# Reordering the edges of an attention stage: two weight loads earlier, the third output's rounding inside the second projection, the first output's columns inside the third

## The chip, the cores and the metric

The kernel runs on one NeuronCore of one Trainium2 chip. The metric is the time of one execution on the device in microseconds (us), as the median of three runs; lower is better. The core's engines work in parallel, each through its own queue in order: TensorE (PE) multiplies matrices and transposes, VectorE (DVE) and GpSimd (POOL) do elementwise arithmetic, ScalarE (ACT) does exponentials and copies and issues some DMAs, and SyncE (SP) issues most DMAs.

## The reference

One transformer block on x (2048 x 512, float32), modulated by a vector c. `A` is an attention with a memory: 32 heads of 16, in 4 segments of 512 rows, causal within a segment, and mixed by `g` with what a linear memory M, z of the earlier segments gives. `B` is a bilinear unit of inner width 1376.

```python
mod = (_silu(c) @ w_mod).reshape(1, 6, 1, -1)
sa, ca, ga, sb, cb, gb = (mod[:, i] for i in range(6))
h = _layernorm(x) * (1 + ca) + sa
x = x + ga * A(h, wq, wk, wv, wo, beta)
h = _layernorm(x) * (1 + cb) + sb
x = x + gb * ((h @ w_gate) * (h @ w_up)) @ w_down
# A, for each segment s with queries qs, keys ks, values vs of each head:
p = _softmax(qs @ ks.T * scale + causal_mask)
o = g * (phi(qs) @ M) / (phi(qs) @ z + 1e-6) + (1 - g) * (p @ vs)
M, z = M + phi(ks).T @ vs, z + phi(ks).sum()
# the segments' o, joined, @ wo
```

## The kernel before

**Precision.** A float32 operand of a projection is split into a rounded high part and the low part that is left (names in H and L: `wkH`, `wkL`, `ahH`, `ahL`, `oH`, `oL`), and three matmuls (high x high, low x high, high x low) make one product. Rounding is a copy on ScalarE, the low part a subtraction on VectorE or GpSimd. Queries and keys are split into three bfloat16 pieces, written to DRAM (`qd`, `kd`) and loaded again in another layout (`qst`, `kst`).

**The attention loop.** The 32 heads are 4 groups of 8, each group two units of 4 heads, so the 4 segments make 32 units u. A turn v of the loop has five slots. In each slot stand a q step of a later unit (scores q on PE, row maxima nm on VectorE), a filling, and a k step of unit v (transposed scores k on PE, exponential pt on ScalarE, and the causal mask on pt as affine selects on GpSimd); in one slot, av_step multiplies the previous unit's pt by v (`tb`), copied out as `tsb` and written to `td`. Later turns load the rows (`orow`) and denominators (`rd`, then `rb`), multiply, add the memory's part `memb` from the second segment on (`o_step`) and write `od`. The maxima nm go through the split nh and the transpose ntp to nt, which a DMA on ScalarE's queue adds to qst before the unit's k steps.

**The filling.** `fill` spends a credit per slot on two generators: `fill_a` (layer norms, weights, projections of queries, keys and values, the memory, the first output projection) and `fill_b` (output projections of segments 1 to 3, the second layer norm's columns, and the first gate and up weights). `weave(a, b, at)` runs a and puts steps of b behind the steps of a that `at` counts. A step that yields a number costs that much credit, and False ends the slot's filling. The instructions' order on PE is written out by hand in this way; most others are pinned behind the PE instruction issued last, and all engines keep the compiled order.

**What the change touches.** `load_g` loads the group g columns of wq or wk (`wrq`, `wrk`) into a staging buffer whose tag `stage` names, and on its second step rounds them. `a_kq` multiplies them with a segment's normalised columns (`kps`, `qps`). `wo_load` loads a segment's od into `orl`; `wo_op` rounds it to `oH` and subtracts to the low part `oL`, in orl's own place; `wo_mm` projects (`wops`), adds x (`xr`) and writes `x1d`. `lnC` loads x1d rows as `x1`, finds mean and factor (`cmv`, `cy`, refined in four small steps on GpSimd), normalises x1 in place and transposes it by columns (`ctp`), which ScalarE copies as `chf`; for the first segment they are split at once (`chH`, `chL`). `prep` loads gate and up weights (`w`) and forms their sums and parts (`AH`, `AL`). The last group of the last segment takes another way, by transposes `tr` of tsb, without DRAM. The first, second and third outputs are the attention outputs of segments 0, 1 and 2 (orl0, orl1, orl2 as loaded), and their rows on the way through projection and second norm. After the loop come the products of the bilinear unit (`g`) and the down projection (`acc`).

## Time and profile before

| | |
|---|---|
| median of 3 runs | 868.59 us (866.88 to 870.31) |
| profiled execution | 865.84 us, of it the span 864.0 us |
| PE busy | 827.9 us, 96% of the span |
| VectorE, ScalarE, GpSimd busy | 652.1, 473.7 and 422.7 us |
| mean granted clock of PE | 0.995 |
| first attention turn to last | about 39 to 505 us |
| products of the bilinear unit, down projection | about 515 us to the end |

The profile is of one execution, on the hardware; times in it are from the start of the span. The page gives busy shares and the chain of work that ended last, followed back from the last instruction. Rows in order of time show the start, the duration, the instruction with what it writes and reads (buffer numbers left out), and in square brackets how long the engine had stood idle and what ended that. PE is full in most stretches, so what counts is where it stands, and what it stands for.

### The profile page before, as it was taken

The numbers are of one execution on the slowest core, as the hardware profiler recorded it, in microseconds if no ns is written. First come the engines' busy times: TensorE is split into PE (matmuls) and PEld (weight loads), VectorE is DVE, ScalarE is ACT, GpSimd is POOL, SyncE is SP. The second block draws the span as 40 slices with busy tenths as digits, with TensorE's granted clock in tenths as the row PEclk, the third lists the DMA queues.
The fourth block names the chain that finished last, engine by engine and source line by source line (L and its number), as shares of the span: only waits on it lengthen the run. The fifth ranks groups of instructions, "written<-read, shape, count | busy, mean of one in ns | idle before, by whom it ended". The sixth has DMA issues, their size and how long they took to land.

```text
span 864.0 us, 14347 instructions
## 1 busy us (share of the span) xinstructions
PE 827.9 (96%) x4823; PEld 580.5 (67%) x4824; DVE 652.1 (75%) x1730; ACT 473.7 (55%) x740; POOL 422.7 (49%) x562
## 2 busy tenths in 40 slices
PE   8979999999999999989997999999999999999998
PEld 5746566556665566555654567888778888887886
DVE  8688678988779777789898878888785667667532
ACT  3747867698668875577545663333364333323321
POOL 4535744577346753586314806998101855550000
PEclk9999999999999999999999999999999999999999
DMA  7773748477566655967894453563315241122032
GB/s 244 233 199 123 229 154 229 151 251 245 159 200 207 214 187 167 271 221 215 253 280 158 148 171 114 168 182 117 107 31 168 74 123 49 50 56 95 0 119 98
DMA packets 111355, 139.45 MB, mean 161 GB/s; under 512 B 18800, under 2 KB 70000, under 8 KB 111280
## 3 DMA queue, kind: packets, MB, share of 16 engines
q1 hardware_dynamic: 106016, 130.91, 49.4%
q10 hardware_dynamic: 5264, 7.62, 2.4%
q8 instruction: 38, 0.62, 0.3%
q14 instruction: 37, 0.30, 0.1%
HBM read 87.48 MB, written 50.76 MB: 160 GB/s over the span
## 4 chain that ended last, share of the span: by engine, by line
PE 70%; DMA 8%; DVE 8%; ACT 6%; POOL 5%; issue 3%; SPq 1%; ACTq 0%; POOLq 0%; DVEq 0%
PE g L90 24%; PE acc L90 14%; PE tb L90 6%; PE k L90 5%; PE q L90 5%; PE vps L90 4%; DVE q L40 3%; PE wops L90 3%; PE kps L90 3%; PE qps L90 3%; ACT pt L338 2%; DMA qd<-q 1%; DMA orl<-od 1%; DMA qst<-nt 1%; DMA memb<-memd 1%
## 5 line engine op out<-in xcount | busy, mean ns | idle before, releaser
L40 DVE CUSTOM_DVE_ANT_0 q<-q,cmask 128x384 f32<-128x384 f32 (+3 forms) x512 | 246.7, 508 | 56.2 <-PE q L90 46.1
L338 ACT ACTIVATE pt<-k 128x1024 f32<-128x1024 f32 x160 | 163.9, 1025 | 66.7 <-PE k L90 54.7
L341 POOL TENSOR_SCALAR_AFFINE_SELECT pt<-pt 128x256 f32<-128x256 f32 (+1 forms) x224 | 106.3, 488 | 143.5 <-ACT pt L338 138.9
L90 PE MATMUL q<-kst,qst 96*128 96x384 bf16 (+3 forms) x512 | 101.3, 300 | 8.4 <-DVE nm L40 7.4
L90 PE MATMUL k<-qst,kst 98*128 98x384 bf16 (+3 forms) x512 | 97.5, 302 | 7.8 <-ACT pt L338 7.3
L457 POOL TENSOR_TENSOR w<-w 128x256 f32<-128x256 f32 (+1 forms) x84 | 72.5, 875 | 65.9 <-DVE t L1228 37.9
L452 POOL TENSOR_TENSOR AL<-w,AH 128x512 fp32r<-128x512 f32 (+1 forms) x42 | 58.8, 1403 | 46.4 <-ACT AH L448 46.4
L90 PE MATMUL tb<-pt,v 128*32 128x512 f32 (+3 forms) x1024 | 75.7, 436 | 0.6 <-POOL pt L341 0.6
L90 PEld LDWEIGHTS <-kst 98*128 98x128 bf16 x512 | 38.2, 99 | 53.1 <-issue 46.0
L40 DVE DVE_READ_ACCUMULATOR2_ANT nm<- 128x1 f32 x512 | 72.1, 141 | 0.0
L448 ACT ACTIVATE AH<-w 128x512 fp32r<-128x512 f32 (+3 forms) x88 | 47.3, 565 | 43.3 <-POOL w L457 30.1
L90 PEld LDWEIGHTS <-qst 96*128 96x128 bf16 x512 | 43.4, 98 | 36.4 <-issue 11.6
L1485 DVE TENSOR_TENSOR mL<-mid,mH 128x512 fp32r<-128x512 f32 (+1 forms) x44 | 32.3, 738 | 41.5 <-ACT mH L1484 41.5
L90 PE MATMUL acc<-DH,mL 128*128 128x512 f32 x144 | 56.6, 393 | 0.9 <-DVE mL L1485 0.9
L90 PE MATMUL acc<-DH,mH 128*128 128x512 f32 x144 | 57.1, 397 | 0.0
L90 PE MATMUL acc<-DL,mH 128*128 128x512 f32 x144 | 56.5, 393 | 0.0
L1484 ACT ACTIVATE mH<-mid 128x512 fp32r<-128x512 f32 (+1 forms) x44 | 27.1, 627 | 51.7 <-PE acc L90 50.5
L90 PEld LDWEIGHTS tb<-pt,v 128*32 128x32 f32 x1024 | 28.6, 109 | 39.3 <-issue 34.5
L1277 ACT ACTIVATE p<-g 128x512 f32<-128x512 f32 (+1 forms) x22 | 13.1, 597 | 74.3 <-PE g L90 74.3
L452 DVE TENSOR_TENSOR AL<-w,AH 128x512 fp32r<-128x512 f32 (+3 forms) x44 | 32.6, 743 | 14.0 <-ACT AH L448 13.9
L367 ACT ACTIVATE tsb<-tb 128x512 f32<-128x512 f32 x32 | 19.1, 596 | 31.8 <-PE tb L90 31.7
L90 PE MATMUL g<-chH,AH 128*128 128x512 f32 (+1 forms) x88 | 34.8, 395 | 0.7 <-ACT p L1277 0.7
(286 smaller groups left out, 2054.6 us busy)
## 6 DMA issues: line engine op xcount, KB each, us to landing
kst<-kd SPq DMA_DIRECT2D x32, 384.0 KB
qst<-qd SPq DMA_DIRECT2D x32, 384.0 KB
td<-tsb ACTq DMA_DIRECT2D x28, 256.0 KB
wm<-in_w_mod_dram SPq DMA_DIRECT2D x24, 256.0 KB
kd<-k SPq DMA_DIRECT2D x16, 384.0 KB
qd<-q SPq DMA_DIRECT2D x16, 384.0 KB
w<-in_w_gate_dram SPq DMA_DIRECT2D x20, 256.0 KB
w<-in_w_up_dram SPq DMA_DIRECT2D x40, 128.0 KB
```

Source lines behind the costliest of these rows:

```text
L40: i = getattr(self.eng, name)(*a, **k)
L90: return pe(nc.tensor.matmul(*a, **k))
L338: lpt[0] = act.activation(pt, kp, AF.Exp, scale=0.25)
L341: sels[u, i] = nc.gpsimd.affine_select(w, w, pattern=[[0, w.shape[1]], [1, P]], compare_op=ALU.is_ge, fill=0.0, base=0, channel_multiplier=-1)
L367: act.activation(tsbs[u], tbs.pop(u), AF.Copy)
L448: i = act.activation(hi[sl], w[sl], AF.Copy)
L452: i = eng.tensor_sub(lo[sl], w[sl], hi[sl].bitcast(F32))
L457: i = ce.tensor_tensor(w[:, o, :, 0:n], w[:, x, :, 0:n], w[:, y, :, 0:n], op=op)
L1277: lcp[0] = act.activation(r["p1"], ps, AF.Copy)
L1484: pin(act.activation(mH[0:n], md[0:n], AF.Copy))
L1485: vec.tensor_sub(mL[0:n], md[0:n], mH[0:n].bitcast(F32))
```

## The change

Four things are changed. The loads of group 3's key and query weights are issued right behind those of group 1, before the attention loop, instead of inside it; the order of staging tags follows, so each weight keeps its buffer's tag. The first key projection of segments 1 to 3 takes all three products of columns 0 to 2 ahead of those of column 3, where it took all low columns last. The segment 3 sum of orow and memb is made by VectorE instead of GpSimd (groups 0 and 1; the two last groups had it there). And `fill_b` is woven anew: the third output's load, rounding and low parts move into the second projection, the low parts from VectorE to GpSimd, and the first output's columns move into the third projection, with the third and fourth columns of each no longer ending a slot.

```diff
--- before.py
+++ after.py
@@ -235,8 +235,6 @@
             if kept_h is not None:
                 kept_h.append(h)
             yield 0.45
-            if pfx == "c" and d % 2 == 1:
-                yield False
         return hH, hL
 
     def run(gen):
@@ -424,7 +422,7 @@
         if i == 0:
             pin(vec.tensor_mul(o, o, rds.pop(ug)))
             if s > 0:
-                nc.gpsimd.tensor_add(o, o, mems.pop(ug))
+                (vec if s == NSEG - 1 else nc.gpsimd).tensor_add(o, o, mems.pop(ug))
             return
         pin(nc.sync.dma_start(od[s][g], o))
         if g == NG - 1:
@@ -486,7 +484,7 @@
         prev = ()
 
         def sub(oL, a, oH):
-            pin(vec.tensor_sub(oL, a, oH.bitcast(F32)))
+            pin((nc.gpsimd if s == 2 else vec).tensor_sub(oL, a, oH.bitcast(F32)))
 
         def half(nm):
             if s % 2 == 0 or g == NG - 1:
@@ -697,7 +695,7 @@
                 i += 1
 
     wH, wL = {}, {}
-    stage = [("ph", 3), ("ph", 3), ("ph", 3), ("mem", 2), ("pkr", 1), ("f", 2)] + [("x", 4)] * 4 + [("mem", 2)] * 2
+    stage = [("ph", 3), ("ph", 3), ("ph", 3), ("mem", 2), ("pkr", 1), ("f", 2)] + [("x", 4)] * 2 + [("mem", 2)] * 2 + [("x", 4)] * 2
     nst = [0]
 
     def staged(nm):
@@ -775,7 +773,7 @@
             ps = bank(f"{nm}ps{s}_{g}")
             terms = [(k, a, b) for k in range(KT) for a, b in ((wH, hH), (wL, hH), (wH, hL))]
             if s > 0 and g == 0 and nm == "k":
-                terms.sort(key=lambda t: t[2] is hL)
+                terms.sort(key=lambda t: (t[0] == KT - 1, t[2] is hL))
             for n, (k, a, b) in enumerate(terms):
                 MM(ps, a[nm, g][:, k, :], b[k], start=n == 0, stop=n == 11)
                 if n in (2, 5, 8):
@@ -1000,10 +998,7 @@
                 ws = []
                 if s == 0 and g == 2:
                     xts[1] = xload(1)
-                if s == 0 and g < 3:
-                    ws = [load_g(nm, w, g + 1) for nm, w in (("k", wk_), ("q", wq))]
-                for w in ws:
-                    next(w)
+                    ws = w3
                 K, Q = a_kq(s, g, "k"), a_kq(s, g, "q")
                 if s == 0 and g == 2:
                     lns = a_ln(1)
@@ -1051,19 +1046,36 @@
         pr = prep(0, "0_0", bc, 1, pb, 1)
         op = wo_op(1, pb, o1, us[1])
         yield from weave(rest, op, (4, 5, 6, 7))
-        B["o0"] = True
-        lg = lnC(0, pb, bc, pb, "x1", 4)
+        lg, o2 = lnC(0, pb, bc, pb, "x1", 4), third(pb)
         rest = weave(wo_mm(1, us[1], xr_load(1, pb, (0,)), pb=pb), chain(op, islice(lg, 10)),
-                     (0, 1, 4, 5, 6, 7, 8, 11, 12, 13, 14))
-        yield from weave(rest, islice(pr, 1), (10,))
+                     (0, 1, 4, 5, 6, 7, 7, 10, 11, 12, 13))
+        rest = weave(rest, chain(o0_free(), islice(pr, 1)), (6, 14))
+        yield from weave(rest, o2, (11, 12, 13, 14, 15))
         while "o2" not in B:
             yield None
-        yield from weave(kept_as("nxt", lg), wo_op(2, pb, B["o2"], us[2]), (0, 1, 2, 3, 3))
+        yield from o2
         B["orl_free"] = True
-        lg = lnC(1, pb, bc, pb, "x1", 4)
-        rest = weave(wo_mm(2, us[2], xr_load(2, pb, (0,)), pb=pb), lg, (0, 3, 4, 5, 6, 7, 10, 11, 12, 13))
-        yield from weave(rest, pr, (1, 8, 9, 14))
-        B["hf"] = yield from lg
+        lh = weaved(kept_as("nxt", lg), pb, bc)
+        rest = weave(wo_mm(2, us[2], xr_load(2, pb, (0,)), pb=pb), lh, (0, 1, 2, 3, 3, 4, 7, 8, 9, 9, 10, 13, 14, 14, 15))
+        yield from weave(rest, pr, (10, 12, 18, 20))
+        B["hf"] = yield from lh
+
+    def weaved(lg, pb, bc):
+
+        yield from lg
+        yield 0.0
+        return (yield from lnC(1, pb, bc, pb, "x1", 4))
+
+    def third(pb):
+
+        while "o2" not in B:
+            yield 0.0
+        yield from wo_op(2, pb, B["o2"], us[2])
+
+    def o0_free():
+
+        B["o0"] = True
+        yield 0.0
 
     def kept_as(nm, g):
         B[nm] = yield from g
@@ -1117,8 +1129,8 @@
         pass
     next(lw[2])
     next(lw[2])
-    w1 = [load_g(nm, w, 1) for nm, w in (("k", wk_), ("q", wq))]
-    for w in w1:
+    w1, w3 = ([load_g(nm, w, g) for nm, w in (("k", wk_), ("q", wq))] for g in (1, 3))
+    for w in w1 + w3:
         next(w)
     run(kq0[1])
     run(kq0[0])
```

SP's queue ahead of the first loads of keys, where wrk and wrq are the weights by group, kd and qd the pieces in DRAM and kst the loaded keys. Before:

```order
L717 DMA wrk1_491<-in_wk_dram 128x4x128
L717 DMA wrq1_495<-in_wq_dram 128x4x128
L805 DMA kd0_0_107<-k3_0_0_478 128x512
L805 DMA kd0_0_107<-k3_0_0_478 128x2x512
L805 DMA kd0_0_107<-k3_0_0_478 128x3x512
L808 DMA qd0_0_91<-q3_0_0_514 128x3x512
L717 DMA wrk2_562<-in_wk_dram 128x4x128
L274 DMA kst0_224<-kd0_0_107 96x2048
L717 DMA wrq2_566<-in_wq_dram 128x4x128
```

Now:

```order
L715 DMA wrk1_491<-in_wk_dram 128x4x128
L715 DMA wrq1_495<-in_wq_dram 128x4x128
L715 DMA wrk3_499<-in_wk_dram 128x4x128
L715 DMA wrq3_503<-in_wq_dram 128x4x128
L803 DMA kd0_0_107<-k3_0_0_478 128x512
L803 DMA kd0_0_107<-k3_0_0_478 128x2x512
L803 DMA kd0_0_107<-k3_0_0_478 128x3x512
L806 DMA qd0_0_91<-q3_0_0_522 128x3x512
L715 DMA wrk2_570<-in_wk_dram 128x4x128
L715 DMA wrq2_574<-in_wq_dram 128x4x128
L272 DMA kst0_224<-kd0_0_107 96x2048
```

Group 3's loads (wrk3, wrq3) stand ahead of all pieces of group 0, and the first kst load stands behind both loads of group 2. Two dozen rows further on, wrk3 and wrq3 are gone from between the loads of qst2 and kst3.

ScalarE's queue around the k steps of units 28 and 29, where orl2 is the third output as loaded and oH2 its rounding, csd0 and cy0 the factor of the first output's rows and chf0 and ctp0 its columns. Before:

```order
L338 ACTIVATE pt28_3_6029<-k28_3_6024 128x1024
L181 ACTIVATE csd0_6010<-cmv0_5898,epst_74 128x4
L183 ACTIVATE cy0_6012<-csd0_6010 128x4
L338 ACTIVATE pt28_4_6056<-k28_4_6051 128x1024
L338 ACTIVATE pt29_0_6083<-k29_0_6080 128x1024
L367 ACTIVATE tsb28_6113<-tb28_6096 128x512
L338 ACTIVATE pt29_1_6120<-k29_1_6117 128x1024
L338 ACTIVATE pt29_2_6143<-k29_2_6138 128x1024
L318 DMA qst2_230<-nt30_6149 2x16x128
L506 ACTIVATE oH2_0_6180<-orl2_0_5848 128x512
L209 ACTIVATE chf0_0_6169<-ctp0_0_6170,modc_83 128x512
L506 ACTIVATE oH2_1_6220<-orl2_1_5850 128x512
```

Now:

```order
L336 ACTIVATE pt28_3_6029<-k28_3_6024 128x1024
L504 ACTIVATE oH2_0_6044<-orl2_0_5993 128x512
L181 ACTIVATE csd0_6004<-cmv0_5890,epst_74 128x4
L183 ACTIVATE cy0_6006<-csd0_6004 128x4
L336 ACTIVATE pt28_4_6055<-k28_4_6050 128x1024
L504 ACTIVATE oH2_1_6068<-orl2_1_5995 128x512
L504 ACTIVATE oH2_2_6078<-orl2_2_5997 128x512
L336 ACTIVATE pt29_0_6088<-k29_0_6085 128x1024
L365 ACTIVATE tsb28_6118<-tb28_6101 128x512
L336 ACTIVATE pt29_1_6125<-k29_1_6122 128x1024
L336 ACTIVATE pt29_2_6155<-k29_2_6150 128x1024
L316 DMA qst2_230<-nt30_6161 2x16x128
```

Three of the four roundings now stand among the exponentials of unit 28, the first of them ahead of csd0, and the first column stands behind pt29_3.

GpSimd's queue around the masks of the last unit, where cyb1, cya1 and cy1 are the steps to the factor of the second output's rows, w0 and AL0 gate and up weights. Before:

```order
L341 AFFINE_SELECT pt30_4_6420<-pt30_4_6420 128x4x128
L452 TENSOR_TENSOR AL0_0_6328<-w0_0_6041,AH0_0_6327 128x512
L188 TENSOR_SCALAR cyb1_6432<-cmv1_6365 128x4
L341 AFFINE_SELECT pt31_0_6452<-pt31_0_6452 128x2x128
L187 TENSOR_TENSOR cya1_6431<-cy1_6429 128x4
L189 TENSOR_TENSOR cyb1_6432<-cyb1_6432,cya1_6431 128x4
L190 TENSOR_SCALAR cyb1_6432<-cyb1_6432 128x4
L191 TENSOR_TENSOR cy1_6429<-cy1_6429,cyb1_6432 128x4
L341 AFFINE_SELECT pt31_1_6477<-pt31_1_6477 128x2x128
L341 AFFINE_SELECT pt31_2_6493<-pt31_2_6493 128x2x128 x2
L341 AFFINE_SELECT pt31_3_6513<-pt31_3_6513 128x2x128 x2
L341 AFFINE_SELECT pt31_4_6542<-pt31_4_6542 128x4x128
```

Now:

```order
L339 AFFINE_SELECT pt31_0_6433<-pt31_0_6433 128x2x128
L339 AFFINE_SELECT pt31_1_6458<-pt31_1_6458 128x2x128
L188 TENSOR_SCALAR cyb1_6476<-cmv1_6414 128x4
L339 AFFINE_SELECT pt31_2_6490<-pt31_2_6490 128x2x128 x2
L450 TENSOR_TENSOR AL0_0_6391<-w0_0_6142,AH0_0_6390 128x512
L187 TENSOR_TENSOR cya1_6475<-cy1_6473 128x4
L339 AFFINE_SELECT pt31_3_6508<-pt31_3_6508 128x2x128 x2
L189 TENSOR_TENSOR cyb1_6476<-cyb1_6476,cya1_6475 128x4
L190 TENSOR_SCALAR cyb1_6476<-cyb1_6476 128x4
L191 TENSOR_TENSOR cy1_6473<-cy1_6473,cyb1_6476 128x4
L339 AFFINE_SELECT pt31_4_6539<-pt31_4_6539 128x4x128
```

The last step to cy1 stood ahead of the mask of pt31_1 and now stands behind the two of pt31_3.

## The prediction

> **What bounds the kernel now.** First the page's sums, to see which engine is full; then the chain of work that ended last, for the places where TensorE is not the bound; then, at those places, the order of time of each engine and the busy time of chosen stretches.
>
> ```profile
> span 864.0 us, 14347 instructions
> PE 827.9 (96%) x4823; PEld 580.5 (67%) x4824; DVE 652.1 (75%) x1730; ACT 473.7 (55%) x740; POOL 422.7 (49%) x562
> ...
> 47.24 7.93 DMA wrk<-in_wk_dram
> ...
> 446.27 7.61 DMA memb<-memd
> ```
>
> TensorE is busy 827.9 of 864.0 us, so 36.1 us of waits is all that a reordering can win, and two of the long pieces of the chain lie where the change works: the load of wrk (the group 3 key weights) at 47 and a load at 446. The change moves work in two stretches: 20 to 68 us, and 440 to 505 us. The profiled execution took 865.84 us (span 864.0 and 1.84 around it); the median shown is 868.59, 2.75 more. I make the sum against the first and carry the difference over to the second. A measurement of this kernel can tell about 0.5% (4.3 us) from no change.
>
> **First stretch: wrk3 and wrq3 load early.** These rows are PE, ACT and DVE in order of time (start, duration, instruction, idle time before it and what ended it), then busy time of stretches (PE, PEld, DVE, ACT, POOL, granted clock, DMA share, GB/s).
>
> ```profile
> 55.19 1.19 ACT L722 ACTIVATE wkH<-wrk 128x512 fp32r<-128x512 f32 x1 [6.18 <-DMA wrk<-in_wk_dram]
> 58.35 0.50 PE L90 MATMUL kps<-ahH,wkH 128*128 128x512 f32 x1 [1.46 <-ACT kf L787]
> 61.87 1.19 PE L90 MATMUL mz<-v,pkr 128*128 128x136 f32 x8 [1.67 <-ACT pkr L868]
> 63.93 1.01 PE L90 MATMUL k<-qst,kst 98*128 98x512 bf16 x2 [0.87 <-ACT pt L338]
> 56.90:68.50 11.60, 7.62 (x38) 4.54 (x38) 8.15 (x28) 8.97 (x15) 8.94 (x13) 0.85 0.41 145
> 58.60:68.10 9.50, 6.97 (x33) 3.89 (x33) 6.11 (x22) 6.90 (x13) 7.24 (x12) 0.82 0.47 166
> 64.00:67.00 3.00, 3.00 (x8) 1.47 (x8) 1.95 (x7) 1.87 (x4) 2.67 (x7) 0.50 0.84 294
> 24.33 0.69 DVE L40 TENSOR_TENSOR kr<-kf,k 128x512 f32<-128x512 f32 x1 [0.23 <-ACT k L40]
> 22.00:23.00 1.00, 1.00 (x4) 0.66 (x4) 1.00 (x2) 0.21 (x1) 0.00 (x0) 0.66 0.03 8
> 39.31 0.61 PE L90 MATMUL q<-kst,qst 96*128 96x512 bf16 x2 [0.43 <-DMA qst<-qd]
> 68.10 0.57 DVE L40 CUSTOM_DVE_ANT_0 q<-q,cmask 128x384 f32<-128x384 f32 x1
> ```
>
> ScalarE stands 6.18 us for the load; behind it in the same queue wait the copies kf and pkr and the exponentials, which is why PE then waits 1.46, 1.67 and 0.87 us. The DMA engines are at 3% at 22 us: the two loads, now issued behind wrk1 and wrq1, run in an empty queue, and the two conversions take their old place in ScalarE's queue with their data long there. What goes: the first wait of PE alone is 1.46 (lower end). In 56.9 to 68.5 PE is busy 7.62 of 11.60, and 3 of those at half clock, worth 1.5: 3.98 + 1.5 = 5.5 is the upper end. What is late next is VectorE: from 58.6 to 68.1 it is busy 6.11 of 9.50, and it has to do the same work, so it lets 3.4 us go. I take 3.4, as the q steps are tied to VectorE on both sides of this stretch. The cost: wrq3 reuses the buffer of wrv1, so SP's queue holds at its issue until VectorE's two wvL subtractions end, just ahead of the kr row at 24.33; the writes of kd (key pieces), ready with the same copy k that this row waits for, then wait for one issue, at most 0.6 us by the issue row further down, and wrq2 now goes ahead of the load of kst0. The same bytes are ahead of the first q step, at 39.31, as before. I book 0.3. Sum of the stretch: -3.1, from -5.5 to -1.2.
>
> **The first key projection of each later segment** takes the low parts of columns 0 to 2 before the last column.
>
> ```profile
> 88.58 0.50 PE L90 MATMUL kps<-ahH,wkH 128*128 128x512 f32 x1 [1.19 <-ACT ahH L231]
> 90.25 0.50 PE L90 MATMUL kps<-ahL,wkH 128*128 128x512 f32 x1 [0.24 <-POOL ahL L232]
> ```
>
> Only here did PE wait in such a projection. Three matmuls fill 0.7 of the 1.19 us, but the last one still waits for GpSimd's ahL at 90.25. I book 0, at best 0.2.
>
> **Second stretch, 440 to 505 us.** Here the load of od2, its rounding oH2 and low parts (on GpSimd instead of VectorE), the transposes of the first output's columns (ctp0) and the third projection (wops2) change places.
>
> ```profile
> 453.95 0.33 ACTq L369 DMA_DIRECT2D td<-tsb  x1
> 454.38 1.02 ACT L338 ACTIVATE pt<-k 128x1024 f32<-128x1024 f32 x1 [3.84 <-DMA memb<-memd]
> 455.45 0.60 PE L90 MATMUL k<-qst,kst 98*128 98x384 bf16 x4 [1.62 <-ACT pt L338]
> 455.99 0.69 DVE L40 BATCH_NORM_STATS2 cst<-x 128x6 f32<-128x512 f32 x1 [1.43 <-DMA x<-x1d]
> 469.63 0.33 PE L93 MATMUL ctp<-ident,x 128*128 128x128 f32 x1 [1.36 <-DVE x L40]
> 470.23 0.66 PE L93 MATMUL ctp<-ident,x 128*128 128x128 f32 x4 [0.27 <-DVE xr L40]
> 473.45 0.60 PE L90 MATMUL k<-qst,kst 98*128 98x256 bf16 x4 [1.25 <-ACT pt L338]
> 475.92 0.59 PE L90 MATMUL k<-qst,kst 98*128 98x512 bf16 x2 [0.55 <-ACT pt L338]
> 476.08 2.89 DVE L40 TENSOR_TENSOR orl<-orl,oH 128x512 fp32r<-128x512 f32 x3
> 472.57 1.27 POOL L232 TENSOR_TENSOR chL<-chf,chH 128x512 fp32r<-128x512 f32 x1 [4.11 <-ACT chH L231]
> 484.30 0.77 POOL L341 TENSOR_SCALAR_AFFINE_SELECT pt<-pt 128x256 f32<-128x256 f32 x2 [0.27 <-ACT pt L338]
> 494.63 0.20 POOL L191 TENSOR_TENSOR cy<-cy,cyb 128x4 f32<-128x4 f32 x1
> 496.17 0.61 PE L90 MATMUL k<-qst,kst 98*128 98x384 bf16 x4
> 498.23 0.63 DVE L40 TENSOR_SCALAR x<-x,cmv,cy 128x512 f32<-128x512 f32 x1
> 498.91 1.26 PE L93 MATMUL ctp<-ident,x 128*128 128x128 f32 x8
> 504.54 0.66 PE L93 MATMUL tr<-ident,tsb 128*128 128x128 f32 x4 [0.63 <-ACT tsb L367]
> ```
>
> The td issue on ScalarE stood for the memb load in a full queue and held the exponentials 3.84 us. With the four od2 loads (1 MB) behind the kst, qst and memb loads this goes: PE gains 1.62 and VectorE 1.43. VectorE spends its share at once, on the sum of orow12 that came over from GpSimd (0.69, by the length of the kr row, the same kind) and on an x normalisation pulled ahead of the q31 steps (0.6); up to the second q31 step it ends where it did. Then three wops2 groups stand where ctp0 waited for x, ScalarE has its exponentials ahead of the columns, and VectorE loses the low parts (2.89 for three, and a fourth). PE's waits of 1.36, 0.27, 1.25 and 0.55 go, 3.4 together. As an estimate, 0.5 of the 1.62 is kept and 0.15 lost where the second ctp0 waits for the first one's column: PE comes to ntp31, the transpose ahead of the last unit's k steps, some 3.8 us early.
>
> That lead meets the second output's columns, ctp1. Each of ctp1's transposes needs x1_1 normalised, with cy1, which GpSimd now finishes behind the masks of pt31_3. The fourth k31 step, at 496.17, ends at 496.62; ctp1 stood 2.3 us behind. In the changed order it is followed by the exponential (1.0), two masks (0.8), three small steps of cy1 (0.2 each and a gap, 0.8) and four normalisations (2.5); ScalarE's AH0 and cy1, ahead of that exponential, may add 0.5: 5.1 to 5.6 us. So ctp1 waits 2.8 to 3.3 us, by the steps' sequence nearer the upper; of the 3.8 gained 0.4 is left at 498.91 with a little for the queues' hand-overs, and the 0.63 at 504.54 goes, as the loads of od3 ahead of that tsb are issued sooner. PE stands wholly idle for those 3.3 us; the nearest such hole is the one at 60.
>
> ```profile
> 60.00:63.50 3.50, 1.40 (x10) 1.02 (x9) 3.37 (x10) 2.77 (x5) 2.28 (x3) 1.00 0.28 100
> 87.00:90.40 3.40, 1.97 (x10) 1.11 (x8) 1.86 (x8) 2.04 (x3) 3.40 (x5) 1.00 0.97 304
> ```
>
> With 1.40 of 3.50 busy the clock then fell to 0.50 for three us; with 1.97 of 3.40 it stayed. An empty 3.3 us is nearer the first: 1.5 of loss with 3 chances in 4, 1.1. [...] Sum: -0.4 - 0.6 + 1.1 = 0.1, booked as 0; the low end is the whole lead and the tr wait, -4.4; the high end is that the lead does not come and the hole stays with its half clock, +3.3 + 1.5 - 0.6 = 4.2.
>
> The sum is -3.1 + 0 + 0: the profiled execution would take 862.7, the median 868.59 - 3.1 = **865.5 us**.
>
> **The rivals.** *The lead is kept:* ctp1 does not wait, as VectorE and GpSimd run ahead of PE there. For it: VectorE is rid of four low parts; against it: the masks of pt31_3 stand ahead of cy1 whatever VectorE does. It decides from a cy1 3 us sooner. -3.1 - 3.8 - 0.6: 861.1; with the upper end of the first stretch 858.7.
>
> *The low parts cost VectorE as much as they free:* the three orl subtractions took 0.96 us each with GpSimd at work beside them, and one alone took 0.69 (the row below). Were each of VectorE's three two-input steps beside the four subtractions on GpSimd (the product and sum of orow12, the split of nm) to stand for a whole one of 1.27, 3.8 us would go and with it the lead: 865.5 + 3.8 = 869.3.
>
> ```profile
> 502.02 0.69 DVE L40 TENSOR_TENSOR orl<-orl,oH 128x512 fp32r<-128x512 f32 x1 [2.57 <-ACT oH L506]
> 452.85 0.58 SPq L418 DMA_DIRECT2D rb<-rdd  x1
> 457.07 0.28 ACT L181 ACTIVATE csd<-cmv,epst 128x4 f32<-128x4 f32 x1
> ```
>
> [...]
>
> *Slower: od2 lands late.* Its loads now stand behind rb12 in SP's queue, and ScalarE takes the first oH2 ahead of csd and the next exponentials. If the queue is as full as before, the first load is issued at 453.4, behind the rb row above, and takes 7.61 as memb did: it lands at 461.0, and ScalarE, there at 457.1, stands 3.9 us, the exponentials and the masks behind it. The hole is long enough for another half clock, 1.5. 865.5 + 5.4: 870.9. It decides from a landing after 457.1, and each us later is one more; 874 where the first stretch gives its lower end too. Against it: with 1 MB fewer ahead of them, the kst and memb loads should end sooner and let these go well before 453.
>
> **How the numbers follow.** Forecast 0.40, lead kept 0.21, low parts 0.15, late od2 0.24. Of the forecast, whose own range is 863 to 868, 0.14 falls below 864.25 and 0.26 within 0.5%; the lead kept is faster, 0.21; low parts 0.13 within and 0.02 above 872.9; late od2 0.08 within and 0.16 above, as its price has no upper end. Faster 0.35, same 0.47, slower 0.18. The range that leaves out two in ten: 860.0 to 872.5.
>
> **What would show it.** Right: no wait of ScalarE for wrk at 55, PE's clock at 1.0 from 62 to 68, the q step of 68.10 about 3 us sooner; no 3.84 ahead of an exponential near 454; no wait of PE for x of ctp0; a wait of PE of about 3 us for x at ctp1, and a clock of 0.5 behind it. Wrong: the first q step (39.3) later by over 0.5 us; ScalarE waiting for orl at oH2; ctp1 without a wait; or the 3 us won at 68 lost again by 93, where a qd load ends a wait.

## The result, and the profile after

The changed kernel takes 871.62 us (median of 10 runs), the kernel before 867.83 us (10 runs): a ratio of 1.0053, with a 95% interval from 1.0031 to 1.0076. That is 3.8 us more where 3.1 us less was forecast, and 865.5 us with a range up to 872.5. The profiled execution of the changed kernel took 868.57 us (span 866.8), that of before 865.84 (span 864.0), so the two traces hold 2.8 of the 3.8 us. Two executions that took two and three times as long, 1635.97 us of the kernel before and 2857.36 us of the run with od2 loaded early, are left out of the medians and ratios.

The head of the page after:

```profile
span 866.8 us, 14342 instructions
PE 830.7 (96%) x4824; PEld 581.2 (67%) x4824; DVE 652.4 (75%) x1728; ACT 474.3 (55%) x740; POOL 422.9 (49%) x564
```

TensorE's busy time grew by 2.8 us although it has the same matmuls. By the clock's records 1.6 of it, as an estimate, is half clock: three stretches of 3.41 us (from 14.30, 461.44 and 502.40) where before had two (from 19.27 and 63.64). The rest stays open. Two pieces of the chain that ended last (start, length, what):

```profile
447.81 8.51 DMA orl<-od
458.56 1.47 DVE x L40
```

In the chain the load of wrk at 47 and that of memb at 446 are gone, and a load of od2 (orl) stands in the place of the second.

Where the time went is seen when the same instruction of TensorE is looked up in both orders of time. Worked out from the two, in us:

```
place                                before    after    shift
first key projection (kps)            18.28    18.72    +0.44   (ahead of anything changed)
first query step                      39.31    40.30    +0.99
ntp1, at the end of the first stretch 67.51    65.09    -2.42
first kps of segment 1, 49th in all   84.85    82.46    -2.39
ntp29                                451.62   449.06    -2.56
first key step behind the tb steps   464.10   465.90    +1.80
ntp31                                483.04   481.30    -1.74
last of the key steps but one        498.46   497.67    -0.79
op                                   503.31   507.67    +4.36
wops, 192nd                          520.74   523.75    +3.01
acc, 503rd                           853.67   856.64    +2.97
```

The first stretch wins 2.9 us in these two traces (from +0.44 to -2.42), near the forecast. The second loses 5.6 (from -2.56 to +3.01), in two holes: 4.4 us by 466, and 5.2 from 498 to 508. Between them 3.5 come back and 1.0 is lost at tb steps that wait for masks; behind the second 1.4 come back.

**First stretch.** PE, ACT, PE and DVE in order of time:

```profile
40.30 0.61 PE L90 MATMUL q<-kst,qst 96*128 96x512 bf16 x2 [0.99 <-DMA qst<-qd]
49.90 1.12 ACT L720 ACTIVATE wkH<-wrk 128x512 fp32r<-128x512 f32 x1
62.72 0.38 PE L90 MATMUL q<-kst,qst 96*128 96x512 bf16 x1 [1.27 <-DVE nm L40]
65.68 0.57 DVE L40 CUSTOM_DVE_ANT_0 q<-q,cmask 128x384 f32<-128x384 f32 x1
```

The busy times from 62 to 68 (PE, PEld, DVE, ACT, POOL, granted clock, DMA share, GB/s):

```profile
62.00:68.00 6.00, 4.75 (x28) 2.91 (x28) 5.71 (x26) 3.23 (x6) 3.10 (x9) 1.00 0.19 65
```

ScalarE no longer waits for wrk (6.18 before), VectorE's query step comes at 65.68 instead of 68.10, VectorE is busy 5.71 of 6 us, and the clock is whole (before, it was halved from 63.64 to 67.05, which is 1.7 of the 2.9). What is late next is VectorE, as it says in the wait of 1.27 for nm. The first query step waits 0.99 for its load instead of 0.43.

The key projection of segment 1, whose terms were sorted anew:

```profile
86.20 0.50 PE L90 MATMUL kps<-ahH,wkH 128*128 128x512 f32 x1 [0.44 <-ACT ahH L231]
87.85 0.49 PE L90 MATMUL kps<-ahL,wkH 128*128 128x512 f32 x1 [0.91 <-POOL ahL L232]
```

The waits were 1.19 and 0.24 and are 0.44 and 0.91: the sum is the same, and GpSimd's ahL ends the second, as forecast.

**First hole, 449 to 466.** SP, ScalarE (ACTq are its DMA issues), VectorE, GpSimd and TensorE in order of time:

```profile
447.81 3.89 SPq L478 DMA_DIRECT2D orl<-od  x4
447.03 0.33 ACTq L367 DMA_DIRECT2D td<-tsb  x1
451.43 0.62 ACTq L316 DMA_DIRECT2D qst<-nt  x1
452.15 1.03 ACT L336 ACTIVATE pt<-k 128x1024 f32<-128x1024 f32 x1 [1.90 <-DVE nm L40]
456.34 0.63 ACT L504 ACTIVATE oH<-orl 128x512 fp32r<-128x512 f32 x1 [3.17 <-DMA orl<-od]
457.31 1.00 ACT L336 ACTIVATE pt<-k 128x1024 f32<-128x1024 f32 x1
456.03 0.69 DVE L40 TENSOR_TENSOR orow<-orow,rb 128x512 f32<-128x512 f32 x1 [1.37 <-DMA rb<-rdd]
458.56 1.47 DVE L40 TENSOR_SCALAR x<-x,cmv,cy 128x512 f32<-128x512 f32 x1 [1.11 <-POOL cy L191]
458.32 0.20 POOL L191 TENSOR_TENSOR cy<-cy,cyb 128x4 f32<-128x4 f32 x1
458.48 1.27 POOL L487 TENSOR_TENSOR orl<-orl,oH 128x512 fp32r<-128x512 f32 x1
458.49 0.61 PE L90 MATMUL k<-qst,kst 98*128 98x512 bf16 x2 [1.95 <-DMA qst<-nt]
461.01 0.38 PE L90 MATMUL q<-kst,qst 96*128 96x256 bf16 x2 [1.91 <-DVE nm L40]
461.92 0.59 PE L90 MATMUL q<-kst,qst 96*128 96x256 bf16 x2 [0.53 <-DVE nm L40]
462.43 3.54 PE L90 MATMUL tb<-pt,v 128*32 128x512 f32 x32
```

And the busy times of three slices there:

```profile
460.00:462.00 2.00, 0.46 (x3) 0.27 (x3) 1.93 (x10) 0.26 (x1) 2.00 (x3) 0.86 0.00 0
462.00:464.00 2.00, 2.00 (x10) 0.42 (x13) 2.00 (x4) 0.00 (x0) 1.52 (x2) 0.50 0.08 30
464.00:466.00 2.00, 2.00 (x29) 0.80 (x22) 1.86 (x10) 0.00 (x0) 0.00 (x0) 0.79 0.80 226
```

The td issue goes at 447.03, so its stall is gone, and TensorE wins 1.57 us by it. But the issue of od2's loads ends at 451.70, the first of them lands at 456.3, and ScalarE, there at 453.2, stands 3.17 us at the first rounding with csd0, cy0 and an exponential behind it: TensorE's wait of 1.95 at a key step is for that exponential (it ends at 458.31, 0.18 ahead of the step; the DMA named was issued 7 us earlier, at 451.43). VectorE meanwhile stands 1.37 for rb12, then 1.11 for cy0 (which stood behind the rounding), and its normalisation of x, 0.63 in the row of before that the prediction shows, takes 1.47 beside GpSimd's low part: TensorE waits 1.91 and 0.53 for the query steps behind it. The three slices show what follows: the clock is halved for 3.4 us (0.56 + 2.00 + 0.84), and the 32 tb matmuls take 3.54 instead of 2.36.

**Second hole, 498 to 508.** VectorE, GpSimd and TensorE in order of time:

```profile
485.75 1.77 DVE L40 TENSOR_TENSOR orow<-orow,rb 128x512 f32<-128x512 f32 x1
489.41 0.69 DVE L40 BATCH_NORM_STATS2 cst<-x 128x6 f32<-128x512 f32 x1
498.66 0.20 POOL L191 TENSOR_TENSOR cy<-cy,cyb 128x4 f32<-128x4 f32 x1
498.89 1.89 DVE L40 TENSOR_SCALAR x<-x,cmv,cy 128x512 f32<-128x512 f32 x3 [1.70 <-POOL cy L191]
499.50 0.33 PE L93 MATMUL ctp<-ident,x 128*128 128x128 f32 x1 [1.22 <-DVE x L40]
500.38 0.78 PE L93 MATMUL ctp<-ident,x 128*128 128x128 f32 x2 [0.55 <-DVE x L40]
501.63 0.33 PE L93 MATMUL ctp<-ident,x 128*128 128x128 f32 x1 [0.47 <-DVE x L40]
503.15 3.66 PE L90 MATMUL tb<-pt,v 128*32 128x512 f32 x32
```

cy1 is made at 498.66 (494.63 before): its statistics start at 489.41, behind the products of orow13 (483.45 before), and its last steps stand behind the masks of pt31_3. The second output's columns wait 2.5 us for their rows in four pieces, the fourth of 0.27 for the sum xr that VectorE does behind them; another 3.4 us at half clock follow. Of the 5.2 us that this hole costs, 2.5 are these waits and 1.7 the half clock; the rest, 0.9, falls on the transposes, which take longer in four pieces (0.33, 0.78, 0.33 and 0.99 us, the last of them partly at half clock, where one piece took 1.26).

### The profile page after: what moved, and what is told of

It is laid out like the page before. It is cut to its first block, busy times and chain, and to the rows that moved or that the text cites. A ratio compares the mean times of both kernels' runs of the same rounds, so it can differ in the third digit from the quotient of the medians.

```text
span 866.8 us, 14342 instructions
## 1 busy us (share of the span) xinstructions
PE 830.7 (96%) x4824; PEld 581.2 (67%) x4824; DVE 652.4 (75%) x1728; ACT 474.3 (55%) x740; POOL 422.9 (49%) x564
## 4 chain that ended last, share of the span: by engine, by line
PE 71%; DVE 10%; ACT 6%; DMA 5%; POOL 5%; issue 2%; SPq 1%; ACTq 0%; POOLq 0%; DVEq 0%
PE g L90 23%; PE acc L90 14%; PE tb L90 6%; PE q L90 5%; PE k L90 5%; DVE q L40 4%; PE vps L90 4%; PE wops L90 3%; PE qps L90 3%; PE kps L90 2%; ACT pt L336 2%; DMA orl<-od 2%; POOL pt L339 1%; PE wups L90 1%; PE mz L90 1%
## 5 line engine op out<-in xcount | busy, mean ns | idle before, releaser
L450 POOL TENSOR_TENSOR AL<-w,AH 128x512 fp32r<-128x512 f32 (+1 forms) x42 | 59.3, 1415 | 46.4 <-ACT AH L446 46.4
L90 PE MATMUL tb<-pt,v 128*32 128x512 f32 (+3 forms) x1024 | 78.4, 446 | 1.2 <-POOL pt L339 1.2
L90 PE MATMUL acc<-DL,mH 128*128 128x512 f32 x144 | 56.5, 392 | 0.0
L365 ACT ACTIVATE tsb<-tb 128x512 f32<-128x512 f32 x32 | 19.1, 596 | 38.9 <-PE tb L90 38.8
```

The lines of the kernel that those rows point to most:

```text
L90: return pe(nc.tensor.matmul(*a, **k))
L365: act.activation(tsbs[u], tbs.pop(u), AF.Copy)
L450: i = eng.tensor_sub(lo[sl], w[sl], hi[sl].bitcast(F32))
```

## The experiments

The theory from these rows: the early loads win what was forecast, and the second stretch loses because ScalarE waits for od2 (first hole), and because cy1 stands late in GpSimd's queue (second hole). The rivals: the low parts on GpSimd slow VectorE; VectorE's order ahead of the query steps; or the early loads bring the second stretch into a bad phase. As the clock adds a run's own noise (its mean is 0.985 to 0.996 over the ten runs of the changed kernel), the table at the end gives the stretches of each profile too. "Before" in a ratio is the kernel before, run on the same chip.

**The first part alone** (kernel before with `w1, w3` loaded together, the new staging order and `ws = w3`).

> The kernel before with the first part alone: wrk3 and wrq3 load behind wrk1 and wrq1, all else as before. If the gain of the first stretch is real and is kept to the end: 2.9 us less than before (the shift of the two traces between the first stages and 68 us), a ratio of 0.9967, no wait of ScalarE for wrk at 55. Rival, the gain of that stretch is spent again at a later wait that is tied to DMAs: within 1 us of before.

Measured: 865.05 us, 0.9960 (0.9939 to 0.9981). There is a gain at the end; what it is made of is asked further down.

**The second stretch alone** (changed kernel with those three edits undone).

> The changed kernel without the early loads: the order of the second stretch and of the key projection alone. If the two stretches add up: 5.5 us more than before (from -2.5 to +3.0 us in the shift of the two traces), a ratio of 1.0064, with the two holes of TensorE near 460 and 502 us. Rival, the second stretch only loses because it is reached 2.5 us sooner: less than 3 us more than before.

Measured: 873.03 us, 1.0063 (1.0038 to 1.0087), both holes at their places. The loss is the second stretch's own; it isn't a matter of reaching it sooner.

**od2 loaded early.**

```diff
-        rest = weave(rest, chain(o0_free(), islice(pr, 1)), (6, 14))
+        B["o0"] = True
+        rest = weave(rest, islice(pr, 1), (14,))
```

> The changed kernel with the four loads of od2 issued where the kernel before issues them; roundings and low parts stay where the change puts them. Theory (od2 lands late, and ScalarE waits at the first rounding with an exponential behind it): no wait of ScalarE for orl, the hole of TensorE at 456 to 462 and its half clock (5.9 us) go, the stall of the td issue (1.6) comes back, so 4.3 us less than the changed kernel, near 867.3; if the wait at the second output's columns grows by as much, 870. Rival (low parts on GpSimd hold the normalisation of x and with it VectorE's query steps): the hole stays at 4 us or more, 870 to 872.

Measured: 870.57 us, 1.0040 (1.0014 to 1.0065). ScalarE and VectorE in order of time:

```profile
455.11 1.02 ACT L336 ACTIVATE pt<-k 128x1024 f32<-128x1024 f32 x1 [3.69 <-DMA memb<-memd]
461.00 1.46 DVE L40 TENSOR_SCALAR x<-x,cmv,cy 128x512 f32<-128x512 f32 x1
```

The first and the last of five slices of 2 us, with a clock of 0.50 in the three between:

```profile
462.00:464.00 2.00, 0.38 (x2) 0.19 (x2) 1.93 (x8) 0.60 (x1) 2.00 (x3) 0.93 0.00 0
...
470.00:472.00 2.00, 2.00 (x10) 1.01 (x8) 1.24 (x3) 1.05 (x2) 0.41 (x1) 0.86 0.89 229
```

ScalarE's wait for od2 is gone and the stall of the td issue is back, both as expected; but the hole stays, by VectorE's chain (orow12, then x beside GpSimd's low part), and this time two windows at half clock follow (0.28 + 6.00 + 0.56 = 6.8 us). The late load was not the whole cause.

**Low parts back on VectorE** (`pin(vec.tensor_sub(...))` for every segment).

> The changed kernel with the low parts of od2 back on VectorE. Theory (late od2): ScalarE still waits 3 us for the load, the hole stays; VectorE's queue now holds four subtractions behind the late roundings as well, so 0 to 3 us more than the changed kernel, 871.6 to 874.6. Rival (GpSimd's low parts are what costs): 3.8 us less, 867.8.

Measured: 873.14 us, 1.0060 (1.0037 to 1.0083): as the theory had it. With the low parts' place alone nothing is won.

**x1_0's normalisation behind the query steps again.**

```diff
-                     (0, 1, 4, 5, 6, 7, 7, 10, 11, 12, 13))
+                     (0, 1, 4, 5, 6, 7, 8, 11, 12, 13, 14))
```

> The changed kernel with one thing put back: the first normalisation of the first output's rows (x1_0) behind the query steps of its turn on VectorE, as in the kernel before; od2 lands as late as in the changed kernel. If the two waits in the hole at 456 to 462 come one behind the other (ScalarE's for od2, then VectorE's for cy0): TensorE's two waits for nm, 1.9 and 0.5 us, shrink to under 0.7 together, its wait of 2 us for the exponential stays, and the time is 2 us less than the changed kernel's 871.6, 4 where a window at half clock goes with it. Rival (all of the hole is the late od2): no change, 871 to 872.

Measured: 870.28 us, 1.0026 (1.0009 to 1.0043), 1.3 us under the changed kernel, with an interval that overlaps its. The waits for nm shrank to 0.16, as expected; the wait for the exponential grew from 1.95 to 2.63.

**Both: od2 loaded early, and x1_0's normalisation behind the query steps.**

> The changed kernel with both put back: od2 issued where the kernel before issues it, and x1_0's first normalisation behind the query steps. If the hole has these two causes and no third: of TensorE's waits between 450 and 464 only the stall of the td issue (1.5) and under 1 us for nm are left, no half clock there; against the changed kernel 4.4 us of waits and 1.7 to 3.4 of half clock less, 1.5 of the stall more: 865 to 867. Rival (low parts on GpSimd slow VectorE by themselves): waits of over 2 us for nm stay, 869 or more.

Measured: 871.93 us, 1.0062 (1.0040 to 1.0083): the expectation failed, waits of 2.1 and 0.5 for nm stayed. The numbers are those of its rival (low parts on GpSimd slow VectorE), but the row shows another cause. VectorE in order of time:

```profile
458.37 1.00 DVE L40 TENSOR_TENSOR orow<-orow,rb 128x512 f32<-128x512 f32 x1 [1.41 <-DMA rb<-rdd]
```

A third wait is left: the product of orow12 stands ahead of the query steps q30_3 and waits for the load of rb12.

**Statistics of the second output's rows sooner.**

```diff
-        rest = weave(wo_mm(2, ...), lh, (0, 1, 2, 3, 3, 4, 7, 8, 9, 9, 10, 13, 14, 14, 15))
+        rest = weave(wo_mm(2, ...), lh, (0, 1, 2, 3, 3, 3, 5, 6, 7, 7, 8, 11, 12, 13, 14))
```

> The changed kernel with the statistics of the second output's rows taken two to three places sooner in the order, so that GpSimd finishes cy1 ahead of two masks that it now stands behind; the first hole stays. If the second hole (waits of 1.2, 0.6, 0.5 and 0.3 us for x at the second output's columns, and one or two windows at half clock behind them) is cy1's place in the queues: 2.5 us and 1.7 to 3.4 less, 866 to 867.5. Rival (GpSimd and VectorE are simply behind there): under 1 us less.

Measured: 867.44 us, 1.0004 (0.9988 to 1.0021), 4.2 us under the changed kernel. At the second output's columns TensorE waits 0.37 and 0.60 in all:

```profile
504.48 0.78 PE L93 MATMUL ctp<-ident,x 128*128 128x128 f32 x2 [0.37 <-DVE x L40]
505.87 0.66 PE L93 MATMUL ctp<-ident,x 128*128 128x128 f32 x4 [0.60 <-DVE xr L40]
```

That the second hole is the place of this chain in the order is shown: TensorE's order is the same, and only the statistics, the steps to cy1 and, on VectorE, the normalisations and sums beside them were moved. The first hole stayed (19.1 us from ntp29 to ntp30).

**Three moves** (x1_0's normalisation; roundings of od2 later; statistics sooner still).

```diff
-                     (0, 1, 4, 5, 6, 7, 7, 10, 11, 12, 13))
+                     (0, 1, 4, 5, 6, 7, 8, 11, 12, 13, 14))
-        yield from weave(rest, o2, (11, 12, 13, 14, 15))
+        yield from weave(rest, o2, (14, 15, 16, 17, 18))
-        rest = weave(wo_mm(2, ...), lh, (0, 1, 2, 3, 3, 4, 7, 8, 9, 9, 10, 13, 14, 14, 15))
+        rest = weave(wo_mm(2, ...), lh, (0, 1, 2, 3, 3, 3, 4, 5, 6, 6, 7, 10, 11, 12, 13))
```

> The changed kernel with three places moved and its other parts kept: od2 still loads late, so that the stall of the td issue stays away, but its roundings start three places later on ScalarE, when it has landed; x1_0's normalisation behind the query steps; the statistics of the second output's rows sooner still than in the run with that move alone. If both holes come from order alone: the early loads' gain (3.5), the td stall (1.6) and the four waits between 469 and 476 (3.4) are kept, 859 to 862, faster than both kernels. Rival (the bound in this stretch is the sum of VectorE's and GpSimd's work): 865 or more.

Measured: 866.36 us, 0.9986 (0.9964 to 1.0008): 5 us under the changed kernel, but not the 859 to 862 of the theory: it lies where the rival has it. ScalarE's issue and VectorE in order of time:

```profile
455.53 0.62 ACTq L316 DMA_DIRECT2D qst<-nt  x1
459.91 0.73 DVE L40 TENSOR_TENSOR orow<-orow,rb 128x512 f32<-128x512 f32 x1 [2.68 <-DMA rb<-rdd]
463.06 0.55 DVE L40 TENSOR_SCALAR x<-x,cmv,cy 128x512 f32<-128x512 f32 x1
```

rb12 again: issued at 450.68, ahead of od2, and used at 459.91. The issue of nt29 stands 2.8 us behind its copy (452.75), with od2's 1 MB in the queues: the stall of the td issue, gone from there, comes back at the next issue. And the normalisation takes 0.55 without GpSimd's low part beside it.

**orow12 a turn later too.**

```diff
-                        if slot == 4:
+                        if slot == 4 and ug != 12:
                             o_step(ug, 0)
+                if v == 29 and slot == 0:
+                    o_step(12, 0)
```

> The run with all three places moved, and one more: the product and the sum of orow12 stand one turn later, behind the query steps q30_3 on VectorE, so that these no longer wait for the load of rb12. If that load (VectorE stood 2.7 us for it, the query steps, the scores and TensorE behind it) is the third cause of the first hole: TensorE's waits of 0.9 and 2.9 us and the window at half clock go, 4 us less than that run's 866.4, near 862. Rival (the stretch is bound by the sum of VectorE's work): 865 or more.

Measured: 863.75 us, 0.9947 (0.9922 to 0.9972), faster than both kernels; the stretch from ntp29 to ntp30 falls from 18.7 to 15.3, and 1.7 of these 3.4 is the half clock that goes. TensorE's waits left in the first hole:

```profile
460.96 0.60 PE L90 MATMUL k<-qst,kst 98*128 98x256 bf16 x4 [1.19 <-ACT pt L336]
464.76 0.60 PE L90 MATMUL k<-qst,kst 98*128 98x512 bf16 x2 [1.32 <-DMA qst<-nt]
```

No window at half clock follows. **Which of the waits leads** was then asked of the changed kernel with single moves: orow12 alone, the roundings alone, both.

> The changed kernel with orow12's product and sum alone moved behind the query steps q30_3; od2's roundings and x1_0's normalisation stay. Between the transposes ntp29 and ntp30, where the kernel before takes 14.8 us and the changed one 19.2: if VectorE's wait for rb12 is the leading cause, 15.5 to 16.5. If ScalarE's wait for od2 leads (csd0 and cy0 stand behind it, and x1_0's normalisation behind cy0), still 18 to 19.

> The changed kernel with od2's roundings alone three places later on ScalarE, behind the load's landing; the product of orow12 and x1_0's normalisation stay ahead of the query steps. From ntp29 to ntp30: if ScalarE's wait for od2 leads, 15 to 16; if VectorE's wait for rb12 leads, still 18 to 19.5, with no wait of ScalarE for orl.

> Both of these moves, and x1_0's normalisation left ahead of the query steps. If the hole is these two waits and the normalisation is a consequence (cy0 comes in time once ScalarE does not wait): 14.5 to 15.5 from ntp29 to ntp30, as in the run with all four moves (15.3). If the normalisation's place is a cause of its own: 16.5 or more.

Measured: orow12 alone 873.09 us, 1.0062 (1.0045 to 1.0080); roundings alone 868.36, 1.0009 (0.9991 to 1.0028); both 867.69, 1.0009 (0.9988 to 1.0029). ScalarE and VectorE with orow12 alone, then VectorE with the roundings alone, then with both:

```profile
460.20 0.63 ACT L504 ACTIVATE oH<-orl 128x512 fp32r<-128x512 f32 x1 [2.89 <-DMA orl<-od]
462.42 1.47 DVE L40 TENSOR_SCALAR x<-x,cmv,cy 128x512 f32<-128x512 f32 x1 [4.78 <-POOL cy L191]
```
```profile
457.60 0.69 DVE L40 TENSOR_TENSOR orow<-orow,rb 128x512 f32<-128x512 f32 x1 [1.47 <-POOL pt L339]
```
```profile
461.25 0.82 DVE L40 TENSOR_SCALAR x<-x,cmv,cy 128x512 f32<-128x512 f32 x1 [1.99 <-POOL cy L191]
```

ScalarE's wait leads: the changed kernel's interval and that of the roundings alone don't overlap, 3.8 us apart by the ratios. In the two profiles, each with one window at half clock in the hole, it is 1.4 us. The granted clock that every run lists tells of the rest: it is 0.9908 in the mean for the changed kernel and 0.9939 for the roundings alone, and 0.0031 of 867 us is 2.7 us at whole clock (an estimate). The stretches from ntp29 to ntp30 are 21.4, 17.7 and 16.4 us, the second between its two forecasts; less 1.7 for each window at half clock they are 18.0, 16.0 and 16.4, against 17.4 in the changed kernel. The move isn't a pure one: GpSimd's low parts go with the roundings, and the normalisation, with none beside it, takes 0.54 in this run instead of 1.47. Without that move, taking rb12 away only makes VectorE stand longer for cy0. Behind it stand rb12 (1.0 to 2.7 where nothing else holds VectorE) and x1_0's place (2.0 for cy0): each keeps the hole open while the other is left, and only with all gone is the stretch as short as before.

**Which engine for low parts and sums,** in the version with all moves: low parts on VectorE, and the sums of orow12 and orow13 on GpSimd.

> The run with all four moves (863.8), with the low parts of od2 on VectorE as in the kernel before. If GpSimd's low parts are a gain once nothing waits for od2: 1 to 3 us more, the steps ntp30 to ntp31 at 15 to 16.6 us instead of 14.2, as VectorE takes 2.9 us for them ahead of query steps. If they slow VectorE by as much as they free: the same, 862.5 to 865.

> The run with orow12 later, with the sums of orow12 and orow13 back on GpSimd as in the kernel before. If VectorE is the one that TensorE waits for at the first output's columns and GpSimd has room there: 0 to 1 us less. If GpSimd's queue (low parts, masks, cy) is the tighter one: 1 to 2 us more, at the second output's columns above all.

Measured: 864.22 us, 0.9961 (0.9941 to 0.9982), and 865.65 us, 0.9973 (0.9952 to 0.9994), each with an interval that overlaps that of the run with all moves (0.9947). TensorE's longest new wait in the one and in the other:

```profile
472.27 0.50 PE L90 MATMUL wops<-woH,orl 128*128 128x512 f32 x1 [1.57 <-DVE orl L40]
```
```profile
496.04 0.64 PE L90 MATMUL tb<-pt,v 128*32 128x256 f32 x8 [1.90 <-POOL pt L339]
```

By these rows both places that the change chose are the better ones; by the times it can't be told.

**The early loads' price and gain.** Behind the writes of kd0 instead of ahead of them (`w3` started behind the second half of `w1`), alone and with all moves:

> The kernel before with the early loads alone, but issued behind the writes of the first key pieces (kd0) instead of ahead of them. If the early loads' price is that wrq3's issue holds the writes of kd0 and so the first query step (0.6 to 1.4 us later by the traces): the first query step is where it was before, 0.9 us less than the run with the early loads alone, a ratio to before of about 0.995. Rival (any megabyte ahead of the first query step costs the same): no difference from that run, 0.996.

> All moves together: the run with orow12 later, with the early loads behind the writes of kd0. If the parts add up: 4.3 us less than before in the first stretch and 2 to 4 in the second, 860 to 862; if a load behind the first query step was not the price of the early loads, the same as the run with orow12 later.

Measured: 865.01 us, 0.9974 (0.9950 to 0.9998), and 862.96 us, 0.9946 (0.9923 to 0.9970). The first query step in the run with the early loads alone, and here:

```profile
40.26 0.61 PE L90 MATMUL q<-kst,qst 96*128 96x512 bf16 x2 [1.27 <-DMA qst<-qd]
```
```profile
40.41 0.61 PE L90 MATMUL q<-kst,qst 96*128 96x512 bf16 x2 [1.15 <-DMA qst<-qd]
```

No difference: that wrq3's issue holds the writes of kd0 isn't the price. What is, stays open; the rival (any such load ahead of the first query step costs as much) fits. Then the kernel before once more, and the best version without the early loads:

> The kernel before itself, unchanged, for a second profile of its first stretch and for what a ratio of 1 looks like. If the profile of before was typical: from the fourth vps matmul to the forty-ninth kps matmul 58 to 59 us, as there (58.5). If it was a slow one, as the run without the early loads suggests (56.5): 56 to 57.5.

> The run with all four moves of the second stretch (0.9947 of before), with the loads of wrk3 and wrq3 back where the kernel before has them. If the early loads gain what the run with them alone showed: 2.5 to 3.5 us more, a ratio of 0.998. If the second stretch alone carries that run's gain: 0.995, no difference.

Measured: 867.03 us, 1.0000 (0.9979 to 1.0022), and 864.72 us, 0.9978 (0.9962 to 0.9994). The second profile of the kernel before has the wait that the change removes:

```profile
55.43 1.15 ACT L722 ACTIVATE wkH<-wrk 128x512 fp32r<-128x512 f32 x1 [6.03 <-DMA wrk<-in_wk_dram]
```

The first stretch takes 57.7 us in it, between the two forecasts. By the times the early loads win 3.5 us alone, 2.3 behind kd0, 2.7 in the best version, and 0.9 between the changed kernel and its second stretch alone: some 2 to 3, not told apart from the 3.1 forecast. By the profiles (first column of the table) the four executions without them take 56.5 to 58.5, 57.5 in the mean, the sixteen with them 55.7 to 59.3, 56.9 in the mean: 0.6. Most of what holds the two apart is the clock. The granted clock is 0.9952 in the mean of the runs with the early loads alone and 0.9929 before, 0.9957 and 0.9927 with the loads behind kd0, 0.9908 in the changed kernel and 0.9880 with its second stretch alone: 0.0023 to 0.0030 more with the early loads, and 0.0023 of 864 us is 2.0 us at whole clock (an estimate). So a gain in time is shown, and most of it is less half clock somewhere in the execution; that the wait for wrk and VectorE's idle time are what it is made of is not shown, and where the clock is won the profiles don't tell.

The profiles, in us: from the 4th vps to the 49th kps matmul; ntp29 to ntp30, with the time at half clock in or right behind the hole; ntp30 to ntp31; ntp31 to op.

```
                                   first    ntp29-30 (half clock)  ntp30-31  ntp31-op
before                              58.5    14.8  (0)              16.6      20.3
before again                        57.7    14.4  (0)              17.5      20.3
early loads alone                   56.6    14.6  (0)              16.5      20.3
early loads behind kd0              56.4    15.2  (0)              16.5      20.3
changed                             55.7    19.2  (3.4)            13.1      26.4
second stretch alone                56.5    20.6  (6.8)            13.1      27.3
od2 early                           57.2    19.5  (6.8)            13.1      27.4
low parts on VectorE                56.4    19.6  (6.8)            14.1      26.0
x1_0 behind                         56.4    18.0  (3.4)            14.2      26.3
both                                56.7    17.9  (0)              14.2      27.4
statistics sooner                   56.8    19.1  (3.4)            13.1      22.3
orow12 alone                        59.3    21.4  (6.8)            13.9      26.5
roundings alone                     56.2    17.7  (3.4)            13.1      26.3
roundings and orow12                58.9    16.4  (0)              13.4      27.4
three moves                         57.7    18.7  (3.4)            14.6      21.2
all four moves                      56.0    15.3  (0)              14.2      21.1
all, loads behind kd0               56.6    14.6  (0)              14.2      21.1
all, low parts on VectorE           56.6    17.5  (3.4)            14.9      21.1
all, sums on GpSimd                 57.0    15.5  (0)              14.6      22.3
all, no early loads                 57.3    17.2  (3.4)            14.2      21.1
```

A window costs a stretch about 1.7 us (half of its 3.41); before again has one in its third column, and the last column has one or two wherever it is over 25.

## Why the prediction was wrong, point by point

**First stretch, -3.1.** It came in this pair of profiles, -2.9, with VectorE as the bound (5.71 of 6 us busy). That its term of 3.4 came to the hundredth (from +0.99 at the first query step to -2.42 behind the stretch) is luck. The term takes all of VectorE's idle time as gone, and with it the half clock that the kernel before had from 63.64 on; but with the early loads a new one mostly stands in its place. The mean gain of the stretch over the profiles is 0.6, and the 2 to 3 us of the times are mostly clock, by the estimate above. The cost of 0.3 was too small: 0.5 in the two traces, and over all profiles the first query step waits 1.4 us in the mean with the early loads (sixteen) and 0.4 without (four). The reason that I gave for it fell. That the clock would be whole from 62 to 68 was right in this execution and wrong as a rule: fourteen of the sixteen profiles with the early loads show a window at half clock that begins between 63 and 67, behind TensorE's new waits for nm, as does one of the four without them. The changed kernel's profile is one of the two that have none, and its 55.7 us is the least of all twenty.

**The sort of the key projection, 0.** Right in the traces: 1.43 us of waits before, 1.35 after. No run has it alone.

**Second stretch, 0, with the lead of 3.8 us at ntp31.** This step failed. At ntp31 the changed kernel was not 3.8 us further ahead, but 0.7 less far than the first stretch had brought it (-2.42 there, -1.74 here). The single gains came: the stall of the td issue (1.57 of the 1.62), the four waits between 469 and 476 (3.5 where 3.4 was forecast), the wait at the tr transposes (0.63). But I added them up as if nothing in between became late next. Three things did. ScalarE's wait for od2 I had as a rival with 0.24 and priced at 3.9; it was 3.17, and by the run with the roundings alone it is worth 3.8 us, most of it as half clock (2.7, by the estimate from the granted clocks). VectorE's wait for rb12 I did not see at all: its product stands in the same row of VectorE's order in both kernels, ahead of the query steps, and in the profile of before the td stall covered it. The second stretch alone is not to blame for it: in the run with only the early loads the same product stands 1.48 us, and TensorE 0.82 and 0.53 for the query steps behind it. And x1_0's normalisation, pulled ahead of query steps, I booked at 0.6 as work; it was 1.47 of work beside GpSimd and a wait of 1.11 for cy0, since I didn't ask who makes cy0 and when.

**The second output's columns, 2.8 to 3.3 us of wait and 1.1 of half clock.** The queue of steps was right (cy1 behind the masks of pt31_3, four normalisations): the wait was 2.5 and the price of the half clock 1.7. But I let the lead pay for it. There was no lead, so all of it was a loss: 5.2 us with the slower transposes, where I had named 4.2 as the high end, and on top of the first hole.

**The rivals.** "od2 lands late" is the nearest, in its mechanism and in its price: 870.9 forecast, 871.62 measured. That the two times lie so near is luck: the first load was issued at 447.81, not 453.4, and took 8.5 us, not 7.61; ScalarE stood there from 453.2, not 457.1; and there were two holes where the rival had one. (Its 874 doesn't follow either: 870.9 with the lower end of the first stretch, 1.9 more, is 872.8.) "Low parts cost VectorE" was half right: not as a whole instruction behind each, but 0.9 us on a normalisation; alone it decides nothing (the run with low parts on VectorE: 1.0060). "The lead is kept" fell. I had asked only for instructions with two inputs, but the normalisation, with one of 128x512, went from 0.55 (three moves) to 1.47 beside a GpSimd subtraction of 1.27, and in the changed kernel a product with two such inputs took 0.69 (orow12) and, beside a GpSimd subtraction of 1.73, 1.77 (orow13): 0.9 and 1.1 us more.

The range held the median, 871.62 under 872.5, but the sign was wrong, and with it the value: the chance of 0.18 for slower was too low for a place where four loads, a rounding and a statistic chain all moved into a stretch in which the DMA queues are full. The row of the kernel before that says so, from 440 to 452.75 (DMA share 0.95):

```profile
440.00:452.75 12.75, 12.19 (x86) 6.90 (x85) 12.03 (x41) 4.67 (x5) 2.66 (x5) 1.00 0.95 286
```

## What to carry to other kernels

When a stall is taken out of a full stretch, write down for each engine what stands next in its queue and when its input lands; the gains of single waits add up only as far as no such input is late, and here three were (a load, a broadcast row, a statistic made on another engine). An instruction pulled ahead in a queue costs its wait and not only its length, and everything behind it pays (x1_0's normalisation: 1.11 us of wait and 1.47 of work, and behind it TensorE's waits of 1.91 and 0.53). A DMA moved later in a full queue need not take the stall away: here it came back in part at the next issue, from td (3.84 us before) to nt (1.3 us behind its copy in the changed kernel, 2.8 in the run with three moves). And where a kernel's runs differ by the clock, compare the granted clock of many runs before a gain is put down to a wait: one profile had the early loads' gain to the hundredth, and twenty profiles have 0.6.

## What the runs showed of the hardware that was not expected

- In the traces of the two kernels the half clock came in stretches of 3.41 us, but for the last of each, which lies behind TensorE's last instruction. By the clock's records they start at 19.27, 63.64 and 862.36 us in the kernel before, and at 14.30, 461.44, 502.40 and 867.63 in the changed kernel: 13 and 234 times 3.413 us apart in the one, 131, 12 and 107 times in the other. Behind the hole at ntp29 the twenty profiles have none of it, 3.4 or 6.8 us (the table), which is 0, 1.7 or 3.4 us of time. Where it falls differs from execution to execution: the two profiles of the kernel before have it at 19 and 64 us, and at 161 and 471.
- The 3.41 us ahead of such a stretch were not idle. TensorE was busy for 0.98 of them ahead of 461.44 and 1.49 ahead of 502.40 in the changed kernel, for 1.19 ahead of 63.64 and 2.52 ahead of 19.27 in the kernel before. In four profiles (before again; roundings and orow12; all, low parts on VectorE; all, no early loads) the mean clock from 160 to 170 us is 0.83 to 0.86; in the changed kernel's and in the first of the kernel before it is 1.00 there, with the same order of TensorE.
- A VectorE normalisation with one input of 128x512 took 1.46 or 1.47 us in five profiles (that of the changed kernel among them, and those of od2 early and orow12 alone) beside a GpSimd subtraction of 1.27 us, and 0.54 or 0.55 with the roundings alone and with three moves, where GpSimd did none.
- The broadcast load rb12 took 8.0 to 9.2 us from issue to use in the six profiles in which VectorE waited for it with od2's 1 MB issued right behind (changed kernel: 447.19 to 456.03; three moves: 450.68 to 459.91). Where od2 is ahead, the same product started 6.1 to 7.9 us after that issue (before: 452.85 to 458.92): the place ahead of od2 did not bring the row sooner here.
